# Decay tables from sigmoids and reciprocals instead of exponentials, with one activation table and a split load for the first k tile alone

## The chip, the cores and the metric

The kernel runs on one core of a Trainium2 chip. A core has a matrix engine (TensorE, PE in the profile, with its weight loads as PEld), three engines for element work (VectorE or DVE, ScalarE or ACT, GpSimd or POOL), a queue processor that issues transfers (SyncE, SP), and 16 DMA engines that all queues share. Each engine works through its own instructions in order and waits on semaphores for the others. The metric is the device time of one execution in microseconds (us), as the median of several runs. The span is the stretch of one profiled execution between its first and last instruction, and is a little shorter.

## What is computed

The inputs are q, k and v of 8 batches, 8 heads, 576 positions and 64 elements per head, and three weight matrices. The first part is attention with a decay in place of a softmax; the second is a gated feed-forward layer over all 4608 tokens:

```python
scores = scale * np.matmul(q, k.transpose(0, 1, 3, 2))
gamma = 1.0 - 2.0 ** (-5.0 - np.arange(H, dtype=np.float32))
Dmat = np.where(rel >= 0, gamma[:, None, None] ** rel[None, :, :], 0.0)
ret = scores * Dmat[None, :, :, :]
attn = np.matmul(ret, v)
gate = 1.0 / (1.0 + np.exp(-(x @ w_gate)))
out = (gate * (x @ w_val)) @ w_out
```

Here `rel` is the query's position minus the key's, and x is the attention's result with the heads laid side by side. As gamma^(i - j) is gamma^i times gamma^(-j), the decay can be put on q and k ahead of the product: each row of q is multiplied by scale times gamma^i and each row of k by gamma^(-j). Two small tables per layout hold these factors: qtab and ktab.

## The kernel before

Work is written out in one hand-made order; no scheduler moves it. Each engine runs its instructions in the order in which the program names them.

**Layout.** The tokens of the first batches are handled in "pairs" (256 tokens each, `PAIRS`), the rest in steps of 128 tokens. For each, q and k are loaded in fp32, multiplied by their table and cast to bf16 (`cast_pair`, line 277, or `cast_qk`, line 290), turned so that the head's elements lie on the partitions, and multiplied. The feed-forward part (lines 731 to 798) follows block by block over 512 tokens, with attention of later steps woven in.

**The start.** The generators of `load_pair` (line 125) issue the loads of pair 0 and 1 in the order k, q, k, q for the two groups of four heads (g = 0 and 1) of each pair, then v; the weights follow. A whole tile is 256 KB. The first k and the first q tile are split over two issuing queues: half on SP, half on ACT (line 130). Meanwhile `fill(10, 4)` (line 191) puts 40 matmuls of a blank tile on TensorE (line 188, named idle).

**The tables.** `tables` (line 192) is called twice: for the pairs ([P, 2, 8, 2], 32 elements per partition; qtab2 and ktab2) and for the steps ([P, 5, 8, 1], 40 elements; qtab and ktab). GpSimd writes the positions with an iota. VectorE multiplies them by log(gamma) with eight small instructions, one per head (line 203). ScalarE then makes ktab as exp(-arg) and qtab as exp(arg + log scale) (lines 204 and 205). Since the gate of the feed-forward part is a Sigmoid, which lies in another activation table than Exp, a one-element Sigmoid (`warm`, line 222) makes ScalarE load that table early. VectorE next clears the four `sbd` tiles (line 227), which later hold block-diagonal states: the first two of pair 0, the last two of pair 1.

**The first steps.** GpSimd casts the k tiles of both pairs (lines 849 to 851) and VectorE the q tiles. For pair 0, group 0, the order at lines 861 to 866 is: q cast, `turn("k")`, `turn("q")`, three filler matmuls, the q cast of group 1, then the score matmuls. A `turn` is four transposes on TensorE (line 317: kTp, qTp) and one copy out of PSUM on ScalarE (line 327: kT, qT). `pair_qk` (line 336: qkp) needs both copies, and VectorE then masks its product into ptp (line 341). The first state matmuls (st, line 372) come after the copies of pair 1.

Of the kernel before, what the change touches and what calls it, by code (L numbers as in the profile page):

```python
# [9 lines left out]
FP32 = mybir.dt.float32  # L10
BF16 = mybir.dt.bfloat16
AF = mybir.ActivationFunctionType
ALU = mybir.AluOpType
# [3 lines left out]
def kernel(  # L17
# [19 lines left out]
    nc = tc.nc  # L37

    B, H, S, D = q.shape
    NT, DM = out.shape  # L40
    DFF = moe_w_gate.shape[1]
    P = 128
    M = H // 2
    NC = (S + P - 1) // P
# [3 lines left out]
    consts = ctx.enter_context(tc.tile_pool(name="consts", bufs=1))  # L48
# [18 lines left out]
    LAST = NC - 1  # L67
# [38 lines left out]
    def half(x):  # L106
        return slice(x * 64, x * 64 + 64)
# [17 lines left out]
    def load_pair(A):  # L125

        b, a2 = PAIRS[A]
        for nm, src, g in (("k", k, 0), ("q", q, 0), ("k", k, 1), ("q", q, 1), ("v", v, 0), ("v", v, 1)):
            t = ld_pool.tile([P, M, 2, D], FP32, tag="ld", name=f"{nm}32p_{A}_{g}")
            queues = (nc.sync, nc.scalar) if A == 0 and g == 0 and nm != "v" else (nc.sync,)  # L130
            n = M // len(queues)
            for i, queue in enumerate(queues):
                queue.dma_start(
                    out=t[:, i * n:(i + 1) * n].rearrange("p h r d -> p h (r d)"),
                    in_=src[b, g * M + i * n:g * M + (i + 1) * n,
                            a2 * 2 * P:(a2 + 1) * 2 * P, :].rearrange("h (p r) d -> p h (r d)", r=2))
            parts[nm, "pair", A, g] = t
            yield
# [11 lines left out]
    def load_wo(f):  # L150
        t = ld_pool.tile([P, DM], FP32, tag="ld", name=f"wo32_{f}")
        nc.sync.dma_start(out=t, in_=moe_w_out[f * P:(f + 1) * P, :])
        parts["o", f] = t

    both = [load_pair(A) for A in range(2)]
    for n_pair in (4, 2):
        for one in both:
# [5 lines left out]
    load_w(4, 4)  # L163
    load_w(8, 4)
    pair_2 = load_pair(2)
    for n_wo, n_pair in ((2, 4), (6, 2), (4, 0)):
        for _ in range(n_wo):
# [16 lines left out]
    def fill(n, parts=1):  # L184

        for i in range(n * parts):
            k = 4 // parts
            nc.tensor.matmul(idle[-1][:, 0:k, :], lhsT=blank, rhs=blank.unsqueeze(1).to_broadcast([P, k, P]),  # L188
                             start=True, stop=True)

    fill(10, 4)
    def tables(shape, pattern, step, put, fix=None):

        pos = consts.tile([P, pattern[0][1], pattern[1][1]], FP32, name=f"pos{step}")
        nc.gpsimd.iota(pos, pattern=pattern, base=0, channel_multiplier=step,
                       allow_small_or_imprecise_dtypes=True)
        if fix:
            fix(pos)
        arg = consts.tile(shape, FP32, name=f"arg{step}")
        qt = consts.tile(shape, FP32, name=f"qtab{step}")  # L200
        kt = consts.tile(shape, FP32, name=f"ktab{step}")
        for h in range(H):
            nc.vector.tensor_scalar_mul(put(arg, h), pos, math.log(1.0 - 2.0 ** (-5.0 - h)))
        nc.scalar.activation(out=kt, in_=arg, func=AF.Exp, bias=0.0, scale=-1.0)
        nc.scalar.activation(out=qt, in_=arg, func=AF.Exp, bias=lnscale, scale=1.0)
        return qt, kt

    lnscale = consts.tile([P, 1], FP32)
    nc.vector.memset(lnscale, math.log(1.0 / math.sqrt(D)))
    qtab2, ktab2 = tables([P, 2, H, 2], [[2 * P, 2], [1, 2]], 2, lambda t, h: t[:, :, h, :])  # L210
    ident = consts.tile([P, P], BF16)
    make_identity(nc, ident)


    def last_chunks(pos):
        nc.vector.tensor_scalar_add(pos[half(1), LAST], pos[half(1), LAST], -64.0)

    qtab, ktab = tables([P, NC, H, 1], [[P, NC], [1, 1]], 1, lambda t, h: t[:, :, h, :], last_chunks)
    qtab = qtab.rearrange("p c h o -> p c (h o)")
    ktab = ktab.rearrange("p c h o -> p c (h o)")  # L220
    warm = consts.tile([P, 1], FP32)
    nc.scalar.activation(out=warm, in_=lnscale, func=AF.Sigmoid)


    sbd = [consts.tile([P, M, P], BF16, name=f"sbd{i}") for i in range(4)]
    for t in sbd:
        nc.vector.memset(t, 0.0)

    trip = consts.tile([P, 2, P], BF16)
# [1 line left out]
    for p0 in (0, 64):  # L231
        nc.gpsimd.affine_select(out=trip[p0:p0 + 64], in_=trip[p0:p0 + 64], compare_op=ALU.is_ge, fill=0.0,
                                base=0, pattern=[[-1, 2], [1, P]], channel_multiplier=-2)
# [30 lines left out]
    def cast_pair(nm, A, g, eng):  # L264

        if (nm, A) not in natural:
            natural[nm, A] = osb_pool.tile([P, 2, H, D], BF16, tag="osb", name=f"{nm}p_{A}")
        if nm != "v" and A == 2:
            o = natural[nm, A].rearrange("p r (m y) d -> p y m r d", y=2)[:, g]
        else:  # L270
            o = natural[nm, A][:, :, g * M:(g + 1) * M, :].rearrange("p r h d -> p h r d")
        i = parts.pop((nm, "pair", A, g))
        if nm == "v":
            eng(out=o, in_=i)
        else:
            tab = (ktab2 if nm == "k" else qtab2)[:, PAIRS[A][1], g * M:(g + 1) * M, :].unsqueeze(3).to_broadcast([P, M, 2, D])
            eng.tensor_tensor(out=o, in0=i, in1=tab, op=ALU.mult)
# [51 lines left out]
    def pair_qk(A, g, banks):  # L329
        ps = [psum.tile([P, 2, 2, P], FP32, tag=tag, name=f"qkp_{A}_{g}_{hh}") for hh, (psum, tag) in enumerate(banks)]  # L330
        for i in range(2):
            m = 2 * g + i
            for r in range(2):
                for a in range(2):
                    for hh in range(2):
                        nc.tensor.matmul(ps[hh][half(a), i, r, :], lhsT=turned["kp", A][half(hh), m, r, half(a)],  # L336
                                         rhs=turned["qp", A][half(hh), m, a * P:(a + 1) * P], start=True, stop=True)
        if g == 0:
            probs["p", A] = [att_pool.tile([P, M, 2, P], BF16, tag="T", name=f"ptp_{A}_{hh}", bufs=6) for hh in range(2)]
        for hh in range(2):  # L340
            nc.vector.tensor_tensor(out=probs["p", A][hh][:, 2 * g:2 * g + 2], in0=ps[hh],  # L341
                                    in1=trip.unsqueeze(1).to_broadcast([P, 2, 2, P]), op=ALU.mult)
# [481 lines left out]
    def turn(nm, A, g, pool=ffn_psum, tag="ffn"):  # L824
        pair_t(nm, A, g, pool, tag, on_act)
# [36 lines left out]
    turn("k", 0, 0, *TR)  # L862
    turn("q", 0, 0, *PV)
    fill(3)
    cast_pair("q", 0, 1, nc.vector)
    pair_qk(0, 0, QK)
    turn("k", 0, 1, *TR)
# [233 lines left out]
```

## Time and profile before

| What | Value |
|---|---|
| median of 3 runs | 328.39 us (328.38 to 328.81) |
| span of the profiled execution | 326.8 us |
| TensorE busy | 317.4 us, 97% of the span |
| VectorE, ScalarE, GpSimd busy | 147.9, 140.7, 104.1 us |
| first table load on ScalarE | 1.87 us, lasts 1.28 |
| second table load on ScalarE | 3.95 us, lasts 1.28 |
| first k cast (GpSimd) | 3.83 to 4.87 us |
| first q cast (VectorE) | 4.50 to 5.41 us |
| first state matmul (line 372) | 12.61 us |

How to read it: the busy shares say which engine has the least room. The times are counted from the start of the span. The chain that ended last is the list of pieces of work that leads, backwards, from the last instruction to the start; what isn't in it had room. A group's line names engine, operation, output and inputs, the shape of one instruction, and the idle time of its engine just before it with what ended it. Ends of matmuls are modelled.

### The profile page before, as it was taken

The numbers are of one execution on the slowest core, as the hardware profiler recorded it, in microseconds if no ns is written. First come the engines' busy times: TensorE is split into PE (matmuls) and PEld (weight loads), VectorE is DVE, ScalarE is ACT, GpSimd is POOL, SyncE is SP. The second block draws the span as 40 slices with busy tenths as digits, with TensorE's granted clock in tenths as the row PEclk, the third lists the DMA queues.
The fourth block names the chain that finished last, engine by engine and source line by source line (L and its number), as shares of the span: only waits on it lengthen the run. The fifth ranks groups of instructions, "written<-read, shape, count | busy, mean of one in ns | idle before, by whom it ended". The sixth has DMA issues, their size and how long they took to land.

```text
span 326.8 us, 8722 instructions
## 1 busy us (share of the span) xinstructions
PE 317.4 (97%) x3584; PEld 170.5 (52%) x3618; DVE 147.9 (45%) x335; ACT 140.7 (43%) x317; POOL 104.1 (32%) x138
## 2 busy tenths in 40 slices
PE   8899999999999999999999999999999999999996
PEld 7664557856546554455445544454445544544443
DVE  6855557656606462355334534344344433404410
ACT  6755545554433353325432553335334533343321
POOL 5774537544364563028200830075003000000000
PEclk9999999999999999999999999999999999999999
DMA  7999999989999999909890899069704810010003
GB/s 218 330 382 376 327 256 243 195 181 168 207 210 192 230 165 239 225 2 221 194 230 0 194 232 224 0 133 225 194 0 121 319 48 0 34 74 27 3 32 96
DMA packets 145849, 55.14 MB, mean 169 GB/s; under 512 B 125200, under 2 KB 137744, under 8 KB 145808
## 3 DMA queue, kind: packets, MB, share of 16 engines
q1 hardware_dynamic: 145120, 54.18, 68.6%
q8 instruction: 28, 0.46, 0.6%
q10 hardware_dynamic: 688, 0.39, 0.4%
q14 instruction: 13, 0.11, 0.1%
HBM read 37.75 MB, written 9.44 MB: 144 GB/s over the span
## 4 chain that ended last, share of the span: by engine, by line
PE 96%; ACT 1%; issue 1%; DVE 1%; ACTq 0%
PE h L731 50%; PE op L798 24%; PE op L980 3%; PE hv L835 3%; PE hg L835 3%; PE val L542 2%; PE idle L188 1%; PE row L516 1%; PE row L524 1%; PE val L558 1%; ACT qT L327 1%; PE op L787 1%; PE hg L906 1%; PE hv L906 1%; PE qkp L336 1%
## 5 line engine op out<-in xcount | busy, mean ns | idle before, releaser
L759 DVE TENSOR_TENSOR gv<-g,h 128x512 bf16<-128x512 bf16 (+1 forms) x96 | 62.8, 654 | 103.2 <-PE h L731 100.5
L731 PE MATMUL h<-xT,wv_sb 128*128 128x512 bf16 (+2 forms) x426 | 100.4, 355 | 0.3
L731 PE MATMUL h<-xT,wg_sb 128*128 128x512 bf16 (+2 forms) x426 | 100.4, 355 | 0.3
L755 ACT ACTIVATE g<-h 128x512 bf16<-128x512 f32 (+1 forms) x96 | 54.7, 570 | 94.3 <-PE h L731 90.2
L798 PE MATMUL op<-wo_sb,gv 128*128 128x512 bf16 x355 | 80.7, 379 | 2.2 <-issue 2.1
L731 PEld LDWEIGHTS <-wg_sb 128*128 128x128 bf16 x432 | 42.0, 98 | 41.2
L731 PEld LDWEIGHTS <-wv_sb 128*128 128x128 bf16 x432 | 42.0, 98 | 40.4
L798 PEld LDWEIGHTS <-gv 128*128 128x128 bf16 x372 | 35.3, 98 | 40.9
L295 POOL CAST v<-v 128x512 bf16<-128x512 f32 x29 | 18.1, 625 | 85.6 <-PE val L542 79.5
L290 POOL TENSOR_TENSOR qk<-k,ktab 128x512 bf16<-128x512 f32 x30 | 31.3, 1042 | 37.0 <-DMA k<-in_k_dram 36.5
L774 ACT COPY ob<-op 128x512 f32<-128x512 f32 x33 | 19.3, 585 | 35.9 <-PE op L798 32.9
L290 POOL TENSOR_TENSOR qk<-q,qtab 128x512 bf16<-128x512 f32 x28 | 29.2, 1042 | 1.9 <-DMA q<-in_q_dram 1.9
L531 DVE TENSOR_TENSOR pt<-row,tri 128x256 bf16<-128x256 f32 x60 | 21.6, 417 | 13.9 <-PE row L524 12.3
L600 ACT CAST xT<-val 128x256 bf16<-128x256 f32 x46 | 15.0, 380 | 22.7 <-PE val L558 18.0
L643 DVE TENSOR_TENSOR s<-s,row 128x256 f32<-128x256 f32 x39 | 16.2, 416 | 1.3
L492 ACT CAST sb<-s 128x256 bf16<-128x256 f32 x44 | 15.9, 420 | 0.3 <-DVE s L643 0.2
L586 DVE COPY glance<-val 128x1 f32<-128x1 f32 x24 | 2.8, 155 | 23.3 <-PE val L558 22.6
L980 PE MATMUL op<-wo_sb,gv 128*128 128x512 bf16 x45 | 11.4, 379 | 0.3 <-issue 0.2
L542 PEld LDWEIGHTS <-v 64*64 64x64 bf16 x480 | 6.2, 108 | 7.5 <-issue 7.2
L558 PE MATMUL val<-T,sb 64*64 64x64 bf16 x368 | 9.7, 195 | 0.3 <-DVE glance L586 0.3
L516 PE MATMUL row<-T 64*64 64x64 bf16 x480 | 9.7, 196 | 0.0
L341 DVE TENSOR_TENSOR ptp<-qkp,trip 128x512 bf16<-128x512 f32 x12 | 7.5, 681 | 3.8 <-PE qkp L336 3.7
(107 smaller groups left out, 236.0 us busy)
## 6 DMA issues: line engine op xcount, KB each, us to landing
out_dram<-ob SPq DMA_DIRECT2D x31, 256.0 KB, 3.1
k<-in_k_dram SPq DMA_DIRECT2D x26, 256.0 KB, 3.9
q<-in_q_dram SPq DMA_DIRECT2D x26, 256.0 KB, 4.1
v<-in_v_dram SPq DMA_DIRECT2D x26, 256.0 KB, 4.5
wg<-in_moe_w_gate_dram SPq DMA_DIRECT2D x12, 256.0 KB, 5.0
wv<-in_moe_w_val_dram SPq DMA_DIRECT2D x12, 256.0 KB, 5.1
wo<-in_moe_w_out_dram SPq DMA_DIRECT2D x12, 256.0 KB, 5.2
v32p<-in_v_dram SPq DMA_DIRECT2D x6, 256.0 KB, 4.9
```

The lines of the kernel that those rows point to most:

```text
L290: eng.tensor_tensor(out=natural_qk[s][:, i].rearrange("p m (y d) -> p y m d", y=2), in0=by_halves(loaded[s][1 - i]), in1=tab, op=ALU.mult)
L295: eng(out=natural["v", s], in_=loaded[s][2])
L492: eng(out=state[key], in_=src)
L531: nc.vector.tensor_tensor(out=probs[s][:, y], in0=row_ps[s][y][:, 0], in1=tri.unsqueeze(1).to_broadcast([P, M, 64]), op=ALU.mult)
L643: nc.vector.tensor_tensor(out=new, in0=running[b], in1=p, op=ALU.add)
L731: nc.tensor.matmul(out, lhsT=w_sb[:, kc, fc * P:(fc + 1) * P], rhs=xT[:, kc, t0 + a:t0 + e], start=(kc == 0), stop=(kc == NKC - 1))
L755: nc.scalar.activation(out=g[:, 0:n], in_=h1[:, 0:n], func=AF.Sigmoid)
L759: nc.vector.tensor_tensor(out=gvs[some[0]][:, a:e], in0=g[:, 0:n], in1=h2[:, 0:n], op=ALU.mult)
L774: (eng or on_act)(out=ob, in_=opp)
L798: nc.tensor.matmul(opp, lhsT=gvs[fc][:, nb * P:(nb + 1) * P], rhs=wo_sb[:, fc, :], start=(fc == 0), stop=(fc == NFC - 1))
L835: nc.tensor.matmul(ps, lhsT=(wg_sb if what == "g" else wv_sb)[:, kc, fc * P:(fc + 1) * P], rhs=xT[:, kc, 0:4 * P], start=(kc == 0), stop=( ...
L980: nc.tensor.matmul(opps[nb], lhsT=gvs[fc][:, nb * P:(nb + 1) * P], rhs=wo_sb[:, fc, :], start=(fc == 0), stop=(fc == NFC - 1))
```

## The change

The tables no longer come from exponentials. With s = Sigmoid(arg) and t = Sigmoid(-arg), s / t is exp(arg) and t / s is exp(-arg). ScalarE makes both sigmoids (they lie in one tile, `both`), VectorE takes one reciprocal of the whole tile (`inv`), and two products give the tables; the scale goes into the q product as a constant. All activations but copies are then Sigmoids, so that one table load is to serve the whole kernel, and `warm` and `lnscale` fall away.

With it the order on VectorE changes. Ahead of the first q cast there now stand: the pairs' arguments, the correction of the steps' positions, four of the eight step arguments, the pairs' reciprocal and products (`tabs2.powers()`), the other four arguments, and two of the four memsets. The steps' reciprocal and products (`tabs1.powers()`) and the other two memsets go between the first and the second q cast. The wait for ScalarE's sigmoids is thus on VectorE, and the first k cast waits for VectorE where it waited for ScalarE.

The first q tile is now issued whole on SP, so that ScalarE issues one transfer ahead of its table load instead of two.

```diff
-            queues = (nc.sync, nc.scalar) if A == 0 and g == 0 and nm != "v" else (nc.sync,)
+            queues = (nc.sync, nc.scalar) if A == 0 and g == 0 and nm == "k" else (nc.sync,)
...
-        for h in range(H):
-            nc.vector.tensor_scalar_mul(put(arg, h), pos, math.log(1.0 - 2.0 ** (-5.0 - h)))
-        nc.scalar.activation(out=kt, in_=arg, func=AF.Exp, bias=0.0, scale=-1.0)
-        nc.scalar.activation(out=qt, in_=arg, func=AF.Exp, bias=lnscale, scale=1.0)
...
+        def args(self, heads):
+            for h in heads:
+                nc.vector.tensor_scalar_mul(self.put(self.arg, h), self.pos, math.log(1.0 - 2.0 ** (-5.0 - h)))
+
+        def sigmoids(self):
+            nc.scalar.activation(out=self.both[:, 0], in_=self.arg, func=AF.Sigmoid)
+            nc.scalar.activation(out=self.both[:, 1], in_=self.arg, func=AF.Sigmoid, scale=-1.0)
+
+        def powers(self):
+            nc.vector.reciprocal(out=self.inv, in_=self.both)
+            nc.vector.tensor_tensor(out=self.k, in0=self.both[:, 1], in1=self.inv[:, 0], op=ALU.mult)
+            nc.vector.scalar_tensor_tensor(out=self.q, in0=self.both[:, 0], scalar=1.0 / math.sqrt(D),
+                                           in1=self.inv[:, 1], op0=ALU.mult, op1=ALU.mult)
+
+    tabs2 = Tables([P, 2, H, 2], [[2 * P, 2], [1, 2]], 2, lambda t, h: t[:, :, h, :])
+    tabs2.args(range(H))
+    tabs2.sigmoids()
+    qtab2, ktab2 = tabs2.q, tabs2.k
...
-    warm = consts.tile([P, 1], FP32)
-    nc.scalar.activation(out=warm, in_=lnscale, func=AF.Sigmoid)
+    tabs1 = Tables([P, NC, H, 1], [[P, NC], [1, 1]], 1, lambda t, h: t[:, :, h, :])
+    nc.vector.tensor_scalar_add(tabs1.pos[half(1), LAST], tabs1.pos[half(1), LAST], -64.0)
+    tabs1.args(range(M))
+    tabs2.powers()
+    tabs1.args(range(M, H))
+    tabs1.sigmoids()
...
-    for t in sbd:
+    for t in sbd[:2]:
         nc.vector.memset(t, 0.0)
...
     turn("q", 0, 0, *PV)
     fill(3)
+    tabs1.powers()
+    for t in sbd[2:]:
+        nc.vector.memset(t, 0.0)
     cast_pair("q", 0, 1, nc.vector)
```

More of the change, by code (lines that the diff above doesn't have):

```diff
@@ L191 @@
     fill(10, 4)
[L192 to L201, printed above, removed]
-        for h in range(H):
-            nc.vector.tensor_scalar_mul(put(arg, h), pos, math.log(1.0 - 2.0 ** (-5.0 - h)))
-        nc.scalar.activation(out=kt, in_=arg, func=AF.Exp, bias=0.0, scale=-1.0)
-        nc.scalar.activation(out=qt, in_=arg, func=AF.Exp, bias=lnscale, scale=1.0)
-        return qt, kt
@@ L208, with __init__, tile_of @@
-    lnscale = consts.tile([P, 1], FP32)
-    nc.vector.memset(lnscale, math.log(1.0 / math.sqrt(D)))
-    qtab2, ktab2 = tables([P, 2, H, 2], [[2 * P, 2], [1, 2]], 2, lambda t, h: t[:, :, h, :])
+    class Tables:
+        def __init__(self, shape, pattern, step, put):
+            def tile_of(name, dims):
+                return consts.tile(dims, FP32, name=f"{name}{step}")
+            self.put = put
+            self.pos = tile_of("pos", [P, pattern[0][1], pattern[1][1]])
+            nc.gpsimd.iota(self.pos, pattern=pattern, base=0, channel_multiplier=step,
+                           allow_small_or_imprecise_dtypes=True)
+            self.arg, self.q, self.k = (tile_of(name, shape) for name in ("arg", "qtab", "ktab"))
+            self.both, self.inv = (tile_of(name, [P, 2] + shape[1:]) for name in ("both", "inv"))
+        def args(self, heads):
[9 more added lines that the diff above has]
+                                           in1=self.inv[:, 1], op0=ALU.mult, op1=ALU.mult)
@@ L211 @@
+    tabs2 = Tables([P, 2, H, 2], [[2 * P, 2], [1, 2]], 2, lambda t, h: t[:, :, h, :])
+    tabs2.args(range(H))
+    tabs2.sigmoids()
+    qtab2, ktab2 = tabs2.q, tabs2.k
     ident = consts.tile([P, P], BF16)
     make_identity(nc, ident)
[L215 to L219, printed above, removed]
@@ L220 @@
-    ktab = ktab.rearrange("p c h o -> p c (h o)")
-    warm = consts.tile([P, 1], FP32)
-    nc.scalar.activation(out=warm, in_=lnscale, func=AF.Sigmoid)
+    tabs1 = Tables([P, NC, H, 1], [[P, NC], [1, 1]], 1, lambda t, h: t[:, :, h, :])
[4 more added lines that the diff above has]
+    tabs1.sigmoids()
+    qtab, ktab = (t.rearrange("p c h o -> p c (h o)") for t in (tabs1.q, tabs1.k))
```

## The prediction, made before the change was run

> **What bounds the kernel now.** I read the shares of the span first, then the chain that ended last, then the same chain for the first 13 us alone, and last each engine's timeline there.
>
> ```profile
> span 326.8 us, 8722 instructions
> PE 317.4 (97%) x3584; PEld 170.5 (52%) x3618; DVE 147.9 (45%) x335; ACT 140.7 (43%) x317; POOL 104.1 (32%) x138
> PE 96%; ACT 1%; issue 1%; DVE 1%; ACTq 0%
> ```
>
> TensorE is busy for 97% of the span and is 96% of the chain. From about 12.6 us on it runs almost without a gap. So the change, which touches only the first microseconds, can move the end only by moving the moment at which that dense stretch begins. What sets that moment is in the chain between 3.9 and 12.6 us (start, length, piece):
>
> ```profile
> 3.90 1.60 PE idle L188 x15
> 5.50 0.44 PE kTp L317 x4
> 5.95 0.02 issue
> 5.97 0.58 ACT kT L327
> 6.55 0.64 ACT qT L327
> 7.19 0.04 issue
> 7.24 0.42 PE qkp L336 x16
> 7.65 0.33 PE kTp L317 x4
> 7.98 0.43 PE idle L188 x2
> 8.41 0.24 PE qTp L317 x4
> ...
> 11.78 0.78 ACT qT L327
> 12.56 0.05 issue
> 12.61 0.39 PE st L372 x4
> ```
>
> There is no table load, no DVE or GpSimd instruction and no transfer in it. It starts with the filler matmuls of line 188 (40 of them, modelled end 5.51 us), goes on through the first transposes, and then alternates between TensorE and the two ScalarE copies of line 327. The tables and first casts lie beside the filler (start, length, engine, instruction, idle before it):
>
> ```profile
> 1.87 1.28 ACT L204 ACT_TABLE_LOAD   x1 [1.87 <-issue]
> ...
> 3.25 1.09 DVE L227 MEMSET sbd<- 128x256 uint32 x4
> ...
> 3.83 1.04 POOL L277 TENSOR_TENSOR kp<-k32p,ktab 128x512 bf16<-128x512 f32 x1 [0.88 <-ACT qtab L205]
> 3.95 1.28 ACT L222 ACT_TABLE_LOAD   x1
> ...
> 4.50 0.91 DVE L277 TENSOR_TENSOR qp<-q32p,qtab 128x512 bf16<-128x512 f32 x1 [0.16 <-DMA q32p<-in_q_dram]
> ...
> 7.10 0.69 DVE L277 TENSOR_TENSOR qp<-q32p,qtab 128x512 bf16<-128x512 f32 x1 [1.69 <-DMA q32p<-in_q_dram]
> ```
>
> What to see: the first k cast ends at 4.87, and the filler still runs until about 5.3 (start of the first transpose) to 5.51 (its own end). So k has about 0.3 to 0.4 us of slack. The page blames the table for the cast's 0.88 us of idle, but ktab was done at 3.39 (the Exp at 3.16 took 0.23). The k halves were issued at 0.80 and landed 2.6 and 2.8 us later, the second at about 3.6. The transfer was the last thing the cast waited for. The second q cast sits behind 1.69 us of empty DVE.
>
> **What the Trainium skill says.** (1) "ScalarE: Activation LUTs", section "What ACT_TABLE_LOAD costs", gives 1283 ns for a load and about 1380 ns of drain on top. The trace shows the 1.28, twice, but no drain: the first Exp starts at 3.16, right behind the load (1.87 + 1.28), and the second load starts at 3.95, right when the last Exp ends (3.64 + 0.31). I use 1.28. (2) "VectorE: DVE Perf Modes", section "First, the fixed hardware budget", says that Reciprocal iterates a divide with a repeat count of 8. The trace has no reciprocal, so whether this means eight cycles per element is open, and this is my upper bound. (3) "DMA: Bandwidth & Descriptors", section "Issuing engines are not separate DMA queues": transfers of SP and ACT run on the same 16 DMA engines, and a second issuing queue saves only issue time. The trace agrees on the price: 0.46 us for half a tile on SP (0.80), 0.47 us for a whole one (1.82).
>
> **The change, part by part.**
>
> *ScalarE.* Its queue loses the q half's issue (1.31 to 1.84). The table load can start at about 1.3 instead of 1.87 and end at 2.6. The arguments of the first tables are ready at 2.04. Two sigmoids at the 0.23 us and 0.14 us spacing of the Exp pair end at about 3.0. Gone are the second load (1.28) and the warm-up (0.20). Both lie before ScalarE's first copy, ahead of which it has been idle for 0.52 us waiting for kTp, so this 1.48 us is worth nothing on the chain. The second sigmoid pair also fits in before 5.97.
>
> *VectorE, ahead of the first q cast.* Two-tensor rows give 417 ns for 256 elements and 680 ns for 512: about 1.03 ns per element and 154 fixed. That makes the reciprocal of 64 elements 0.22 us and each product of 32 elements 0.19. At eight cycles an element of 0.96 GHz (that page's clock) the reciprocal would be an estimated 0.15 + 0.53 = 0.68. I take the low price and keep the high one for the range. DVE finishes the first four arguments at about 2.76, waits for ScalarE until about 3.05, then reciprocal and k product follow each other: ktab at about 3.5 (high: 3.95), qtab at 3.6 (4.05). Queued behind that wait are four arguments (0.125 each, from eight in 1.00 us), two memsets (0.27 each) and the q cast; it starts at 3.6 + 0.5 + 0.54 = 4.65 instead of 4.50 (high: 5.1). One memset pair was taken out ahead of it, but the three new operations and the wait cost about as much.
>
> *The first k cast.* It waits for the later of ktab (3.5, high 3.95) and k's second half (3.6). It starts at about 3.8 as before, at 4.05 in the high case, and ends at 4.85 to 5.1. The filler hides it both times: gain 0, loss 0. The filler's length isn't touched, so an earlier ktab buys nothing.
>
> *The first q cast and the qT copy.* At 0.68 to 0.91 us it ends at 5.33 to 5.56, against 5.41. The qT copy can't begin before the kT copy lets it, at 6.45, and qTp was over at 5.72 + 0.45 = 6.17. So 0.28 us is spare behind qTp, with another 0.2 ahead of it. At the low price nothing is lost; at the high one the cast ends at about 6.0, qTp at 6.6, and the chain loses some 0.17.
>
> *VectorE, between the q casts.* Reciprocal of 80 elements (0.24), two products of 40 (0.20 each) and two memsets (0.54): 1.2 us from about 5.5, done by 6.7 and hidden by the 1.69 us gap ahead of the second q cast at 7.10. At the high price it is 1.8 us from 6.0: the cast starts at 7.8 instead of 7.10 and ends at 8.5 instead of 7.79. Its transpose started at 8.25, so the loss is some 0.3. The idle filler of line 188 and the chain's wait for qkp absorb the rest.
>
> *The q load on one queue.* SP issues the first q in 0.47 instead of 0.46 us, so no later load is issued later. The bytes are the same. In quarter-microsecond windows the rate falls to 166 to 252 GB/s between 4.25 and 5.25, while only SP's queue has work, against 307 to 346 between 3.0 and 3.75 with both busy. If that dip came from having one queue, it would now start up to 0.8 us earlier: 100 GB/s for 0.8 us is 80 KB, or 0.25 us at 330 GB/s on every later load. Against that, q no longer shares the engines with the k tile queued behind it. The second k and q casts end 0.4 us before their transposes start (7.14 against 7.59, 7.79 against 8.25). The tightest is the k cast of pair 1, half 1: its transposes end at 11.25 against an ACT start of 11.31. I take 0, with up to 0.2 for the range.
>
> Sum, likeliest: 0 us; bounds: 0 to about +0.7 (0.17 + 0.3 + 0.2).
>
> **The rivals.**
>
> *Slower, 329.2.* The reciprocal iterates, DVE becomes the limit of the first two steps, and the load dip starts earlier: 0.17 + 0.3 + 0.2 = 0.67 and, say, 0.1 for DVE and GpSimd working at once at 6.10 (the q cast at 4.50, beside a k cast, took 0.91 against 0.69 for the next one). For it: DVE is now in the middle of the path from arguments to q cast, with no spare between 3.05 and 5.5. Against it: 32 to 80 elements is little, and after 10 us the ScalarE copies set the pace.
>
> *Faster, 327.6.* The chain's head isn't really held by the filler. Ends of matmuls are modelled, so the first transpose could be waiting for the casts, or the missing table load and the q tile's better order could bring the loads forward. ScalarE gains about 0.55 us at the front, and q could land 0.2 earlier: 0.75 in all. Against it: no wait is shown ahead of the first kTp weight load at 5.19, and the k transfer landing at 3.6 caps the cast's start at about where it is.
>
> **How the numbers follow.** No measurable change has a chance of 0.65, slower 0.18 (bounds of an unmeasured reciprocal and transfer, all to that side), faster 0.17 (a kernel so tightly laid out can reorder its small waits later, and my slack is a difference of modelled times). The time is that of the likeliest: 328.4, the time before. The range takes in part of both rivals: 327.6 to 329.2, from 328.39 minus 0.8 to plus 0.8. The 0.2% bound is 0.66 us, so 327.7 to 329.05 counts as the same; only the outer ends of the bounds leave it.
>
> **What would show it.** Right: one table load starting near 1.3; the first k cast still near 3.8; the first kTp still at about 5.3 behind the filler; the qT copy still at about 6.45; the first state matmul (line 372) still near 12.6. If the reciprocal is dear, it lasts about 0.7 us and the second q cast starts after 7.1 with no wait for its transfer. If the queue matters, the casts' waits for k and q transfers grow. Wrong: a first state matmul shifted by more than 0.6 us either way, or a shift that arises after 13 us, in the stretch that I take as fixed.

## The result and the profile after

The changed kernel takes 331.64 us (median of 6 runs, 330.25 to 332.18) against 328.39: a ratio of 1.0092, 95% interval 1.0071 to 1.0113. It is slower by about 3 us, and outside the range that I gave.

The span and the first queue's line of the page after (packets, megabytes, the time its packets took as a share of the 16 engines' span):

```profile
span 330.2 us, 8760 instructions
...
q1 hardware_dynamic: 145376, 54.31, 76.5%
```

The same queue before:

```profile
q1 hardware_dynamic: 145120, 54.18, 68.6%
```

So 224.2 us of packet time (0.686 x 326.8) became 252.6 us (0.765 x 330.2) for the same bytes plus one half tile: about 12.5% more per packet on average, over the whole kernel. It isn't every packet. By the traces' records of single packets, 98% of the 256-byte packets before took at most 20 ns; after, 70% did, and most of the rest took 21 to 35. Of the 512-byte packets, 99% before and 58% after took at most 29 ns, while those of 2048 bytes took 92 ns on average in both.

No line of the diff touches the later loads. The windows of the kernel after show the slower stream from 8 us on (window; busy time and count of PE, PEld, DVE, ACT, POOL; clock, DMA share, GB/s):

```profile
8.00:12.00 4.00, 3.44 (x43) 1.68 (x41) 3.32 (x7) 2.57 (x5) 2.19 (x2) 1.00 1.16 293
12.00:16.00 4.00, 3.36 (x88) 2.57 (x88) 3.61 (x6) 2.48 (x5) 2.46 (x4) 1.00 1.16 293
```

The same windows before:

```profile
8.00:12.00 4.00, 3.75 (x59) 2.25 (x57) 3.51 (x6) 3.08 (x6) 2.71 (x3) 1.00 1.12 335
12.00:16.00 4.00, 3.39 (x102) 2.79 (x103) 3.19 (x6) 2.67 (x7) 3.22 (x6) 1.00 1.10 325
```

The DMA engines are no less busy (share 1.16 against 1.12 and 1.10; it adds up the packets' times, and can pass 1), but move 293 GB/s instead of 335 and 325. The chain of the kernel after begins differently too:

```profile
...
7.41 5.52 DMA v32p<-in_v_dram
12.94 0.05 issue
12.99 0.63 POOL vp L285
13.61 0.04 issue
13.66 0.49 PE st L383 x6
```

Where the filler and the ScalarE copies stood, there now are SP's load issues, up to 7.37, and a v transfer. And TensorE, which I had taken to run without a gap from 13 us on, waits later in the kernel (waiting engine, for whom: us in total, times, longest):

```profile
PE row L527 <- DMA T<-qk: 1.5, 2, 1.1
PE qTp L328 <- DVE qp L288: 1.0, 3, 0.7
```

The first line, two waits at 69 and 75 us for the transposing transfers that SP issues behind its loads, isn't in the profile before. (The second is for the late q casts of the first 13 us.) The gate matmuls of line 846 begin at 22.35 us (line 835 before: 21.06), so 1.29 us is lost by then and 1.50 in these two waits, of 3.4 us of span. The remaining 0.6 us I have not placed.

VectorE's first stretch in the kernel after:

```profile
2.99 0.55 DVE L214 RECIPROCAL inv<-both 128x64 f32<-128x64 f32 x1
...
3.79 1.26 DVE L207 TENSOR_SCALAR arg<-pos 128x5 f32<-128x5 f32 x4
3.91 1.12 POOL L288 TENSOR_TENSOR kp<-k32p,ktab 128x512 bf16<-128x512 f32 x1 [0.96 <-DVE qtab L216]
...
5.05 0.55 DVE L238 MEMSET sbd<- 128x256 uint32 x2
...
5.51 0.62 DVE L288 TENSOR_TENSOR qp<-q32p,qtab 128x512 bf16<-128x512 f32 x1
...
6.06 0.63 DVE L214 RECIPROCAL inv<-both 128x80 f32<-128x80 f32 x1
...
6.73 0.76 DVE L215 TENSOR_TENSOR ktab<-both,inv 128x40 f32<-128x40 f32 x1
```

Two costs are to be seen that I had not put there. The reciprocals take 0.55 and 0.63 us. And four arguments that cost 0.5 us together in the kernel before take 1.26: they end only when GpSimd's k cast ends (3.91 + 1.12 = 5.03).

### The profile page after: what moved, and what is told of

It is laid out like the page before. It is cut to its first block, busy times and chain, and to the rows that moved or that the text cites. A ratio compares the mean times of both kernels' runs of the same rounds, so it can differ in the third digit from the quotient of the medians.

```text
span 330.2 us, 8760 instructions
## 1 busy us (share of the span) xinstructions
PE 320.9 (97%) x3618; PEld 169.5 (51%) x3618; DVE 149.9 (45%) x340; ACT 139.3 (42%) x315; POOL 104.8 (32%) x138
## 4 chain that ended last, share of the span: by engine, by line
PE 91%; DMA 4%; SPq 2%; DVE 1%; ACT 1%; issue 0%; POOL 0%; ACTq 0%
PE h L742 50%; PE op L809 23%; PE op L994 3%; PE hg L846 3%; PE hv L846 3%; DMA T<-qk 2%; SPq L133 2%; PE val L553 2%; DMA v32p<-in_v_dram 2%; PE row L527 1%; PE val L569 1%; PE row L535 1%; PE op L798 1%; PE hg L920 1%; PE hv L920 1%; PE st L383 0%
## 5 line engine op out<-in xcount | busy, mean ns | idle before, releaser
L809 PE MATMUL op<-wo_sb,gv 128*128 128x512 bf16 x372 | 84.0, 379 | 0.0
L994 PE MATMUL op<-wo_sb,gv 128*128 128x512 bf16 x48 | 11.7, 379 | 0.0
L846 PE MATMUL hg<-xT,wg_sb 128*128 128x512 bf16 x40 | 9.2, 379 | 0.0
```

The costliest lines, as they stand in the source:

```text
L809: nc.tensor.matmul(opp, lhsT=gvs[fc][:, nb * P:(nb + 1) * P], rhs=wo_sb[:, fc, :], start=(fc == 0), stop=(fc == NFC - 1))
L846: nc.tensor.matmul(ps, lhsT=(wg_sb if what == "g" else wv_sb)[:, kc, fc * P:(fc + 1) * P], rhs=xT[:, kc, 0:4 * P], start=(kc == 0), stop=( ...
L994: nc.tensor.matmul(opps[nb], lhsT=gvs[fc][:, nb * P:(nb + 1) * P], rhs=wo_sb[:, fc, :], start=(fc == 0), stop=(fc == NFC - 1))
```

## The experiments

**What else had changed.** The constants come first in the memory of a partition, and the pool of load tiles right behind them. In the compiled program the new tiles `both` and `inv` add 1152 bytes and two small tiles fall away (64 bytes with their padding), so all that follows moves by 1088 bytes: the load tiles start at byte 98624 instead of 97536. The old start is 381 x 256; the new one is 64 past a multiple of 256. The Trainium skill has a matching statement in "DMA: Bandwidth & Descriptors", section "How a descriptor splits into AXI transactions": a transfer that doesn't start on a multiple of 256 bytes can be cut into more pieces. It says so of reads; here it would be the writing side in SBUF. So my theory became: the shifted addresses make the loads slow. Rivals: the single queue for q; VectorE's dear work. Four kernels separate them.

**The changed kernel, aligned again.** The two inverse tiles share one room, and unused bytes bring the start to 98560 = 385 x 256.

```diff
+    inv_room = consts.tile([P, 2 * NC * H], FP32, name="inv")
...
-            self.both, self.inv = (tile_of(name, [P, 2] + shape[1:]) for name in ("both", "inv"))
+            self.both = tile_of("both", [P, 2] + shape[1:])
+            self.inv = inv_room[:, :2 * math.prod(shape[1:])].rearrange("p (s a h r) -> p s a h r", s=2, a=shape[1], h=H)
...
     glance = consts.tile([P, NJ], FP32)
+    consts.tile([P, 48], FP32, name="spare")
```

> The changed kernel, with its two inverse tiles laid into one shared room (256 bytes less) and 192 unused bytes put at the end of the constants, so that the load tiles start at byte 98560 of a partition, a multiple of 256, instead of 98624, which is 64 past one. Instructions and their order stay. Address theory (the new table tiles pushed every load tile off a multiple of 256 bytes, and transfers into them got slower): the time returns to about 328.5, between 328.0 and 329.2, and the load rate between 8 and 16 us returns from 293 to about 330 GB/s. Queue theory (the first q load on one queue slows the stream): 331 to 332, rate 293. VectorE theory (the dear reciprocals and the moved work delay the first steps): 330.5 to 332.

Measured: 329.36 us, ratio to the kernel before 1.0027 (1.0019 to 1.0035), and the waits for the T transfers are gone. The median lies just above the band I gave. The packets are back near their old share:

```profile
q1 hardware_dynamic: 145376, 54.31, 69.1%
```

Some 70% of the loss goes away with the address. The rest, about 0.9 us, doesn't.

**The kernel before, 64 bytes on.**

```diff
     glance = consts.tile([P, NJ], FP32)
+    consts.tile([P, 16], FP32, name="spare")
```

> The kernel before, with 64 unused bytes at the end of its constants, so that the load tiles start 64 bytes past a multiple of 256; nothing else. Address theory: slower by 2 to 3.5 us, 330.5 to 332, load rate between 8 and 16 us near 293 GB/s. Queue theory and VectorE theory: 328.4, rate near 330.

Measured: 331.61 us, ratio 1.0091 (1.0072 to 1.011). Sixteen unused floats per partition cost as much as the whole change. Added to the 1.0027 of the aligned kernel it makes 1.0118, more than the change's 1.0092; the intervals leave open whether the two losses overlap in the changed kernel or the sum is chance. Its windows, with not one instruction different from before:

```profile
8.00:12.00 4.00, 3.64 (x59) 2.12 (x57) 3.00 (x6) 3.07 (x6) 2.48 (x3) 1.00 1.17 290
12.00:16.00 4.00, 3.30 (x116) 2.62 (x104) 3.06 (x5) 2.31 (x6) 2.34 (x5) 1.00 1.17 294
```

and its page's queue line and one wait of TensorE:

```profile
q1 hardware_dynamic: 145120, 54.18, 76.9%
```

```profile
PE row L516 <- DMA T<-qk: 1.0, 1, 1.0
```

The rate, the packets' share and the later of the two waits are those of the changed kernel.

**The queue part alone, in the kernel before and undone in the changed one.**

```diff
-            queues = (nc.sync, nc.scalar) if A == 0 and g == 0 and nm != "v" else (nc.sync,)
+            queues = (nc.sync, nc.scalar) if A == 0 and g == 0 and nm == "k" else (nc.sync,)
```

> The kernel before, with only the queue part of the change: the first q tile issued whole on SP. Load tiles stay on multiples of 256 bytes. Address theory: 328.0 to 328.9. Queue theory: 330.5 to 332, load rate near 293 GB/s. VectorE theory: 328.4.

> The changed kernel with its queue part undone: the first q tile is split over SP and ACT again; the load tiles stay 64 bytes past a multiple of 256. Address theory: 330.5 to 332.5, no better than the changed kernel. Queue theory: 328.2 to 329. VectorE theory: 331 to 332, as ScalarE's table load also starts later again.

Measured: 328.70 us, ratio 0.9999 (0.999 to 1.0007), and 330.92 us, ratio 1.0078 (1.006 to 1.0096). The queue costs nothing that can be measured, and undoing it doesn't clearly help. The queue theory falls.

**Which tiles.** Only the load tiles are shifted in the first of these two (their pool is put last, behind 64 unused bytes), only the pools behind them in the second.

```diff
-    ld_pool = ctx.enter_context(tc.tile_pool(name="ld", bufs=18))
...
     osb_pool = ctx.enter_context(tc.tile_pool(name="osb", bufs=13))
+    ctx.enter_context(tc.tile_pool(name="spare", bufs=1)).tile([P, 16], FP32, name="spare")
+    ld_pool = ctx.enter_context(tc.tile_pool(name="ld", bufs=18))
```

> The kernel before, with the pool of load tiles put last and 64 unused bytes ahead of it: only the load tiles start 64 bytes past a multiple of 256, all other pools keep their remainder. If the loads are what the shift costs: 330.7 to 331.9, load rate between 8 and 16 us near 293 GB/s. If the transposing transfers into the T tiles or the stores are: 328.3 to 329.2, rate near 330.

```diff
     ld_pool = ctx.enter_context(tc.tile_pool(name="ld", bufs=18))
+    ctx.enter_context(tc.tile_pool(name="spare", bufs=1)).tile([P, 16], FP32, name="spare")
```

> The kernel before, with 64 unused bytes behind the pool of load tiles: loads stay on multiples of 256, all later pools (cast tiles, T tiles, output tiles) are 64 bytes past one. If the loads carry the cost: 328.2 to 328.9. If the T tiles or the stores carry it: 329.5 to 331.5, with waits of row matmuls on the T transfers.

Measured: 331.00 us, ratio 1.0079 (1.0051 to 1.0107), for the load tiles, and 328.66 us, ratio 1.000 (0.999 to 1.001), for all others. The same window in the first and then in the second:

```profile
8.00:12.00 4.00, 3.35 (x57) 1.98 (x56) 2.91 (x6) 2.93 (x6) 2.47 (x3) 1.00 1.17 291
```

```profile
8.00:12.00 4.00, 3.81 (x61) 2.30 (x58) 3.79 (x6) 2.95 (x6) 3.41 (x4) 1.00 1.16 348
```

The loads carry the whole cost. The first of the two kernels also moves their pool to the other end of the partition; but the kernel with 64 bytes behind its constants leaves the pool in its place and is as slow, and the second clears all pools but this one. The T tiles' own address costs nothing that can be measured.

Where TensorE then waits is not fixed. With the load tiles alone shifted there is no wait for T, but one at 45 us for the casts of v tiles:

```profile
PE st L356 <- POOL vp L275: 1.3, 2, 0.7
```

So the waits for T are one place at which slow loads can show, and not a part of the cause. That they come from SP issuing the transposes behind slower loads fits, but no run tests it alone.

**Twice the shift.**

```diff
     glance = consts.tile([P, NJ], FP32)
+    consts.tile([P, 32], FP32, name="spare")
```

> The kernel before with 128 unused bytes at the end of the constants. If any start off a multiple of 256 costs the same (each 512-byte packet then touches three blocks of 256 instead of two): 330.7 to 332, rate between 8 and 16 us near 293 GB/s, as with 64. If only a start off a multiple of 128 costs: 328.2 to 329.

Measured: 331.24 us, ratio 1.007 (1.0042 to 1.0098), 295 and 291 GB/s in the two windows. A start on a multiple of 128 isn't enough. That both remainders cost the same fits packets that touch one more block of 256 bytes each; the trace doesn't show the blocks themselves, and as most small packets took no longer, a fixed price for each packet isn't what it shows. The two good starts, 97536 and 98560, lie 1024 bytes apart, so by themselves they don't tell 256 from a larger unit. But a step's load tile holds rows of 256 bytes, one on every multiple of 256, and with aligned tiles 98% of the 256-byte packets took at most 20 ns. That fits the 256 of the skill's page and not a larger unit.

**The rest, 0.9 us.** In the aligned changed kernel the chain runs through VectorE:

```profile
2.99 0.56 DVE inv L217
3.58 0.19 DVE ktab L218
3.77 0.10 DVE qtab L219
3.87 0.53 DVE arg L210 x4
4.40 0.62 issue
5.01 0.27 DVE sbd L241
...
5.56 0.55 DVE qp L291
6.11 0.57 DVE inv L217
6.70 0.97 DVE ktab L218
...
8.32 0.55 DVE qp L291
...
8.92 0.41 PE qTp L331 x4
```

The "issue" of 0.62 us has no releaser, but GpSimd's k cast runs from 3.91 to 4.99, and the next memset starts at 5.01; the product of 40 elements, worth 0.20, takes 0.97 while the second k cast runs from 6.56 to 7.60. The Trainium skill describes this in "SBUF — State Buffer", section "SBUF: two separate sides": VectorE and GpSimd share one pair of ports, which a GpSimd instruction or a VectorE one of certain kinds (with two inputs in SBUF, or in a two-port mode) holds for its whole length. The trace agrees for arguments and products. The memsets of the kernel before ran at 0.27 each beside its first k cast (3.83 to 4.87). The first run clears VectorE's path by order alone, the next two vary the queue and the reciprocals:

```diff
-    tabs1.args(range(M))
+    tabs1.args(range(H))
     tabs2.powers()
-    tabs1.args(range(M, H))
...
     tabs1.powers()
-    for t in sbd[2:]:
-        nc.vector.memset(t, 0.0)
     cast_pair("q", 0, 1, nc.vector)
+    for t in sbd[2:]:
+        nc.vector.memset(t, 0.0)
```

> The aligned changed kernel with another order on VectorE: all eight step arguments ahead of the first reciprocal, and the last two memsets behind the second q cast, so that nothing but two memsets (no input) stands between the first products and the first q cast. Theory (in the aligned kernel the four arguments and a product of VectorE stood blocked behind GpSimd's k casts, 0.62 and about 0.8 us, and with them both q casts): the first q cast ends near 5.7 instead of 6.1, the second near 7.9 instead of 8.87, the first state matmul moves from 13.39 to about 12.6, and the time to 328.3 to 328.8. Rival (the residue of 0.75 us in the aligned kernel is the dear reciprocals themselves, 0.55 and 0.63): no better than 329.2.

Measured: 329.34 us, ratio 1.0025 (1.0013 to 1.0037), a miss. The order did what it was to do (the first q cast ends at 5.64, the second starts at 7.77 instead of 8.24), but in the profiled run the second q cast and the third k cast then waited for their transfers, 0.99 and 1.96 us, and the first state matmul stayed at 13.48. That run moved 293 GB/s between 8 and 16 us with aligned tiles, but this isn't the address at work: the DMA share was 1.00, not 1.16, and 98% of its 256-byte packets took at most 20 ns. The engines were less busy, not slower. Its 14 times spread from 328.67 to 330.39, with the profiled one at 330.00. Why the loads of this run came late stays open.

> The aligned changed kernel with the first q tile split over two queues again. Theory (what is left of the loss, 0.75 us, is VectorE's work ahead of its q casts): no gain, 329.2 to 329.9, as ScalarE's table load and with it the reciprocals start 0.5 us later. Rival (with the sigmoid tables the single queue does cost): 328.4 to 328.8.

Its edit is that of the queue part, undone. Measured: 329.58 us, ratio 1.0028 (1.0018 to 1.0038): no gain, as expected. The table load starts at 1.86 again, and the first k cast at 4.45 instead of 3.91.

```diff
-            nc.vector.reciprocal(out=self.inv, in_=self.both)
+            nc.vector.tensor_scalar_mul(self.inv, self.both, 2.0)
```

> The aligned changed kernel with a product by 2 in the place of each reciprocal: it leaves out the inverse, so that its tables are not the decay factors; all else stays. Theory (the two reciprocals, 0.55 and 0.63 us where I had put 0.22 and 0.24, are the mis-sized term): the first products end near 3.5, the first q cast moves at most 0.1 to 0.3 earlier because it also stands behind the first k cast, the second q cast comes 0.4 to 0.9 earlier, and the time is 328.5 to 329.0. Rival (the blocked small instructions and the loads are the cause, not the reciprocals): 329.2 to 329.5.

Measured: 329.05 us, ratio 1.0003 (0.9991 to 1.0015); the median is a shade above the band. The product of 64 elements takes 0.20 us where the reciprocal took 0.55, so the four arguments are through at 3.82, just after the k cast starts (3.75), and cost 0.38 together:

```profile
3.00 0.20 DVE L217 TENSOR_SCALAR inv<-both 128x64 f32<-128x64 f32 x1
...
3.44 0.38 DVE L210 TENSOR_SCALAR arg<-pos 128x5 f32<-128x5 f32 x4
3.81 0.55 DVE L241 MEMSET sbd<- 128x256 uint32 x2
4.41 0.93 DVE L291 TENSOR_TENSOR qp<-q32p,qtab 128x512 bf16<-128x512 f32 x1
```

The residue is gone within the interval: the reciprocals are its cause. How much of it is their own length and how much is what they push behind the k cast isn't separated. In the two runs ahead of this one the four arguments no longer waited for the cast (they stood ahead of it, or took 0.38 together), and the residue stayed.

**Towards a better version.** All arguments and all four memsets ahead of the first q cast; the steps' reciprocal and products, needed only by the later steps, first at about 20 us, then in VectorE's gap at 39 us. The cuts show only this last move.

```diff
     first_sum()
+    tabs1.powers()
```

> The aligned changed kernel with VectorE's first stretch cleared: all arguments ahead of the first reciprocal, all four memsets (not held up by GpSimd) ahead of the first q cast, and the steps' reciprocal and products moved to about 20 us, behind the sum of the first states. Theory (VectorE's extra work ahead of the q casts is the residue): second q cast starts as soon as its load has landed, time 328.0 to 328.8. Rival (slower loads beside the new tables are the residue): 329.0 to 329.5.

```diff
     loads_to(1)
+    tabs1.powers()
```

> As the aligned kernel with late powers, but the steps' reciprocal and products stand in VectorE's idle gap of 3.7 us at about 39 us, where no gate product waits behind them. Theory (VectorE's extra work on the path is the residue, and the move to 20 us only shifted it ahead of a gate product, where TensorE waited 0.4 us): 328.2 to 328.9, level with the kernel before or a little better. Rival (loads beside the new tables, or the later start of the first k cast, are the residue): 329.2 to 330.

Measured: 329.93 us, ratio 1.0038 (1.0027 to 1.005), a miss, and 328.81 us, ratio 1.0011 (1.0004 to 1.0018), in its band. In the first, the reciprocal and products start at 22.42 us and delay a gate product for which TensorE then waits 0.4 us. That profile is of the fastest of its 22 executions (329.03), so what the median loses beyond it stays open. In the gap at 39 us the work is hidden; the second q cast starts as soon as its transfer lands:

```profile
6.93 0.89 DVE L290 TENSOR_TENSOR qp<-q32p,qtab 128x512 bf16<-128x512 f32 x1 [1.30 <-DMA q32p<-in_q_dram]
...
12.36 0.62 PE L385 MATMUL st<-vp,kp 64*128 64x128 bf16 x8 [0.49 <-ACT qT L340]
```

The first state matmul is even 0.25 us earlier than in the kernel before, yet the median is a little above it. The last 0.1% stays open. No version here beats the kernel before.

## Why the prediction was wrong, point by point

**The step that failed** is the sum, "likeliest: 0 us; bounds: 0 to about +0.7". I summed the parts that the diff names. The largest term, some 2 to 3 us, isn't among them: the change moves all later tiles in SBUF, and with "The bytes are the same" I took the loads to cost the same. Moving the load tiles by 64 bytes alone gives 1.0079, moving them with all that follows 1.0091. The smaller term, VectorE's, was in the sum with its likeliest value at 0 and measured about 0.9 us.

**"Can move the end only by moving the moment at which that dense stretch begins"** was wrong as well. TensorE's 97% hid that the loads were the next limit: with slower loads, waits of 1.5 us opened at 69 and 75 us. I had named such a shift after 13 us as what would prove me wrong. The other sign, a first state matmul more than 0.6 us late, was just about reached (13.21 for 12.61).

**The q load on one queue**: right, 0.9999, and the rival that the load dip starts earlier falls. The dip from 4 to 5 us comes with one queue (260 and 252 GB/s in the two halves, in the kernel before with one queue) and with two (214 and 191).

**ScalarE**: right; the table load starts at 1.31 and the second is gone. The earlier start is worth nothing that can be measured: in the aligned kernel, 1.0028 without it and 1.0027 with it. For the second load no run tests this alone.

**VectorE**: the mechanism was right, the size wrong. The mis-sized term is the reciprocal: 0.55 and 0.63 us measured, 0.22 and 0.24 taken, 0.68 and about 0.82 the upper ends. By the two durations it is 5 ns per element (81 ns for 16 more) and about 0.23 us fixed. The Trainium skill's repeat count of 8 ("VectorE: DVE Perf Modes", section "First, the fixed hardware budget") pointed to the right end without being the measured slope. And I let the four arguments pass beside the k cast for free. The sign I had named for a dear reciprocal came true: the second q cast started at 8.07, after 7.1, with no wait for its transfer. My high case for this chain, about 0.5 us (0.17 + 0.3), or 0.6 with the slower rival's 0.1 for VectorE and GpSimd at once, is somewhat less than the aligned kernel shows: a gate matmul start 0.79 us late, 0.27% in time.

**The first k cast**: start right (3.91 for 3.8). "The filler hides it both times" didn't hold in this profile: the filler ended at 4.77, not at 5.51, and the first transpose then waited 0.31 us for the cast, though it still began at 5.08, ahead of the 5.3 before. The filler's length, which I took as fixed, lies between 3.70 and 4.45 us in the profiles of kernels that don't touch it.

**The slower rival** had the right side, but for reasons that explain less than a third of it (0.9 of about 3 us).

## What to carry to other kernels

A new constant tile is a change to every address behind it. Before you cost an edit that adds or drops tiles, compare the start of the pool that loads write, modulo 256, in both compiled programs, and keep it on a multiple. The other pools didn't matter here. When packets get slower though no transfer was edited, look at addresses as well as queues. A lower load rate alone is not the sign: one aligned run had it too, with packets as quick as ever. And a matrix engine at 97% doesn't mean that the transfers have room.

## What the runs showed of the hardware

- Loads into tiles that start 64 or 128 bytes past a multiple of 256 ran at 289 to 295 GB/s from 8 to 16 us, where the aligned ones of the kernel before reach 335 and 325. The first queue's packets took 74.3 to 78.5% of the engines' span in the five shifted kernels, 68.1 to 69.5% in the nine aligned ones.
- The small packets carry it: 67 to 78% of the 256-byte packets took at most 20 ns in the shifted kernels, 96 to 98% in the aligned ones. Packets of 2048 bytes took 91 to 95 ns on average in both.
- On VectorE a reciprocal of 64 fp32 elements per partition took 0.553 us, of 80 elements 0.634; a product by a constant of 64 took 0.20.
- Small multiplications by a constant (four took 1.26 us instead of 0.5) and a two-input product (0.97 instead of 0.20) on VectorE stood still while GpSimd's k cast ran. Memsets (0.27 each) and, with the arguments ahead, the reciprocal of 80 elements (0.64, beside a cast from 5.57 to 6.61) didn't.
- A switch to another activation table cost its load of 1.28 us and no more: in the kernel before, the load begins at 3.95, when the activation ahead of it ends, and the next one starts at 5.25.
